# PSUM banks by lists, another order of maxima, and six smaller moves in a transformer block of one core

## The chip, the cores and the metric

The kernel runs on one core of a Trainium2 chip. The metric is the time of one execution in device microseconds (us), as the median of several runs. TensorE (PE) multiplies matrices into PSUM, which has eight banks of 128 rows by 512 float32; VectorE (DVE) and ScalarE (ACT) read PSUM; GpSimd (POOL) works on SBUF alone; SyncE (SP) issues the DMAs from one queue.

## The reference

One block of a transformer in float32 for 2048 tokens of width 640: layer norm and attention with 32 heads of 20, then layer norm and a gated feed-forward layer of width 1728, both with a residual.

```python
h  = x + attention(layernorm(x), wqkv, wo)   # qkv = z @ wqkv; softmax(q k^T / sqrt(20)) v; @ wo
h2 = h + (silu(z2 @ w_gate) * (z2 @ w_up)) @ w_down   # z2 = layernorm(h)
```

## The kernel before

Tokens go in 4 chunks (`NC`) of 512, each of 4 tiles of 128. Products are exact in two parts: `split` writes the high part of a tensor with ScalarE (`hi`, type fp32r) and the rest with another engine (`lo`); three products `hi*hi`, `hi*lo`, `lo*hi` are added. The program's order on each engine is written out by the Python code; there is no scheduler behind it. All waits between engines follow from which tiles are read and written.

**First phase, projections.** For each chunk `c` the work list has "block" steps (128 columns of q or k, 15 products twice, once for each half of 64 rows of the array, which run side by side) and "value" steps. Each step has a number, the slot; `begins(c)` is the first slot of a chunk, and the list has 72 slots. Between the products the planner `Halves` places *pairs*: parts of the row maxima of q k^T, which attention needs before it takes exponentials. They lie in two lists. `early` holds maxima of units 2, 4, 5, 8 and so on that can be had from the projected chunks; `others` holds those of units 0 and 1. A unit `u` is 4 heads (`g = u // 4`) by one chunk of queries (`c = u % 4`), 32 units in all. `staged_keys` makes 8 pairs for a set with one key tile and 16 for one with two; `early` gets 240 pairs and `others` 48, in the order unit 0, unit 1, unit 0, unit 0. A set's keys and queries are loaded back from DRAM into free places, those of `others` in a lane of their own (`lane=1`) with two places. `next_pair` says which list is asked first. When the last pair of unit 0 is issued, `over` calls `max_all(0)` (DVE L242, POOL L246 and L247); `max_finish(0)` (PE L254, ACT L258, four DMAs L263) writes the maxima as two more rows of the queries. It runs two slots after that (`finish_at`), or, where the list of slots ends before, behind `pe.drain()` and the last load of values (L170). `norm(c)` makes the layer norm of a chunk (L720 applies it), `flip` transposes it (L745).

**Attention.** For each unit, 16 key tiles. `ORDER` is the order of one tile: `s` and `S` are scores of a head in the lower and upper half of the array (L1336, then the exponential, L1342, on ScalarE), `m` and `M` a maximum of a later unit (L229 and DVE L235), `W` the weighing of the tile before (`weigh`, L1346), which uses four strips of 32 columns. Steps of other work stand behind `W`: weight preparation, and in the last two units the output projection of chunks 0 and 1 (`projection`; its parts: `part`, L89, splits the attention output `o_t` into `o_hi` and `o_lo`; `project`, L1070, 15 products of 128x320, added to `h` at L1076; `apply`, L1090; `flip`, L1102, five transposes, then `split`). Its PSUM comes from `ps_max`, three banks. The planner knows when maxima end (`closing`), so that `max_finish(u)` comes some tiles before unit `u`.

**After attention.** The last unit's sums are normalised: ACT L1356 copies the accumulator, a reciprocal (L1367), `r_d` and back as `rb`, a product (L1381), stores to `o_d`. Meanwhile chunk 2 is projected (`two`), then chunk 3 (`three`), which loads `o_d` again. Then the feed-forward layer runs over 14 weight blocks (`ELEMENTS`) for two pairs of chunks: `blocks` gives the gate and up products (L1514) of PSUM `ps_a`; between its 8 steps, `next_down` issues the down projection of earlier blocks (L1608, PSUM `ps_b`), a `Group` of 7 or 4 products at a time. `prepare` splits a group's input into `yp`, one of three buffers. `late_tokens` normalises, transposes (L1861, L1878) and stores chunks 2 and 3, one item a step.

PSUM is handed out by tile pools, closed and opened again at four places: `psum_f` (the first transposes), `psum` (first phase: `ps_one` 3 banks, `ps_single` 5), `psum_a` (attention: `ps_one` 4, `ps_max` 3, `acc` 1), `psum2` (`ps_b` 4, `ps_a` 4).

Of the kernel before, what the change touches and what calls it, by code (L numbers as in the profile page):

```python
# [17 lines left out]
P = 128  # L18
# [22 lines left out]
MARGIN = 0.2  # L41
LAST_QUARTER = 60
# [5 lines left out]
def tile_block(ctx: ExitStack, tc: tile.TileContext, x, wqkv, wo, wg, wu, wd, out):  # L48
# [20 lines left out]
    ps_ctx = ExitStack()  # L69
    psum = ps_ctx.enter_context(tc.tile_pool(name="psum_f", bufs=1, space=bass.MemoryType.PSUM))  # L70
    wides, ones = 3, 1

    def ps_wide():
        return psum.tile([P, 2, CH], F32, name="ps_wide", tag="ps_wide", bufs=wides)

    def ps_one():
        return psum.tile([P, CH], F32, name="ps_one", tag="ps_one", bufs=ones)

    def ps_single():
        return psum.tile([P, CH], F32, name="ps_single", tag="ps_single", bufs=5)  # L80
# [248 lines left out]
    with tc.tile_pool(name="pa", bufs=2) as pa:  # L329
# [184 lines left out]
        class Halves:  # L514
# [32 lines left out]
            def issue(self, half):  # L547
# [3 lines left out]
                if half == 0 and i == 0:  # L551
                    del self.ones[0]
                    job["ps"] = ps_one()
# [14 lines left out]
                if job["at"][1] == job["n"]:  # L568
                    self.jobs.remove(job)
                    self.ones.append(job["done"](job["ps"]) + 0.2)  # L570
# [143 lines left out]
        def norm(c):  # L714
# [4 lines left out]
            def apply(t):  # L719
                (nc.gpsimd if c else nc.vector).tensor_scalar(  # L720
# [10 lines left out]
                + [(("pool", 1.3), lambda t=t: apply(t), c) for t in range(TPC)]  # L731
# [137 lines left out]
        ps_ctx.close()  # L869
        ps_ctx = ExitStack()  # L870
        psum = ps_ctx.enter_context(tc.tile_pool(name="psum", bufs=1, space=bass.MemoryType.PSUM))
        ones = 3
# [118 lines left out]
    ps_ctx.close()  # L991


    ps_ctx = ExitStack()
    psum = ps_ctx.enter_context(tc.tile_pool(name="psum_a", bufs=1, space=bass.MemoryType.PSUM))

    def ps_one():
        return psum.tile([P, CH], F32, name="ps_one", tag="ps_one", bufs=4)

    def ps_max():  # L1000
        return psum.tile([P, CH], F32, name="ps_max", tag="ps_max", bufs=3)
# [36 lines left out]
    def projection(c, ps_of):  # L1038
# [17 lines left out]
        def part(t):  # L1056
# [3 lines left out]
            split(o, o_hi, o_lo, nc.gpsimd)  # L1060
            loaded[t] = (o_hi, o_lo)

        def project(t, half):
            o_hi, o_lo = loaded[t]
            hs = slice(half * HALF, (half + 1) * HALF)
            ps = ps_of()
            n = 0
# [981 lines left out]
```

## Time and profile before

| | |
|---|---|
| median of 3 runs | 2039.87 us (2039.75 to 2042.74) |
| the profiled execution | 2035.66 us, span of its instructions 2033.9 us |
| TensorE busy | 2008.8 us (99%) |
| VectorE, ScalarE, GpSimd busy | 1612.6, 1462.4, 785.7 us |
| mean granted TensorE clock | 0.997 |
| first phase, to the first score at | 328.1 us |
| attention, to the last weighing at | 1470.1 us |
| DMA | 305.03 MB, mean 150 GB/s |

Times in the profile are from the first instruction. A busy TensorE is not TensorE at its peak: its matmuls are pipelined, and their ends are modelled. Rows of the timeline read: start, duration, engine, line, operation, output<-input, shape, count, and in brackets the idle time of the engine just before and what ended it. Rows of waits read: who waited, for whom, total us, times, longest.

### The profile page before, as it was taken

The numbers are of one execution on the slowest core, as the hardware profiler recorded it, in microseconds if no ns is written. First come the engines' busy times: TensorE is split into PE (matmuls) and PEld (weight loads), VectorE is DVE, ScalarE is ACT, GpSimd is POOL, SyncE is SP. The second block draws the span as 40 slices with busy tenths as digits, with TensorE's granted clock in tenths as the row PEclk, the third lists the DMA queues.
The fourth block names the chain that finished last, engine by engine and source line by source line (L and its number), as shares of the span: only waits on it lengthen the run. The fifth ranks groups of instructions, "written<-read, shape, count | busy, mean of one in ns | idle before, by whom it ended". The sixth has DMA issues, their size and how long they took to land. (4 is left out here: it accounts for less than half of the span.)

```text
span 2033.9 us, 39129 instructions
## 1 busy us (share of the span) xinstructions
PE 2008.8 (99%) x13716; PEld 1238.9 (61%) x13716; DVE 1612.6 (79%) x3241; ACT 1462.4 (72%) x2952; POOL 785.7 (39%) x1079
## 2 busy tenths in 40 slices
PE   7999999999999999999999999999999999999999
PEld 6899996333333333333333333345598888888888
DVE  6678788888888888888888888885377666676677
ACT  3788988999999999999999999987633222211221
POOL 5554450334434334344430011011145454744555
PEclk9999999999999999999999999999999999999999
DMA  7776663343443534444433123211158654974642
GB/s 227 243 222 186 203 185 100 113 128 99 150 124 113 163 123 138 129 141 146 141 126 109 30 65 80 83 62 49 41 193 292 222 193 156 346 272 159 202 151 95
DMA packets 205124, 305.03 MB, mean 150 GB/s; under 512 B 47664, under 2 KB 82480, under 8 KB 203904
## 3 DMA queue, kind: packets, MB, share of 16 engines
q1 hardware_dynamic: 204832, 302.53, 45.9%
q8 instruction: 109, 1.79, 0.4%
q14 instruction: 87, 0.71, 0.1%
q10 hardware_dynamic: 96, 0.00, 0.0%
HBM read 205.78 MB, written 95.68 MB: 148 GB/s over the span
## 5 line engine op out<-in xcount | busy, mean ns | idle before, releaser
L1342 ACT ACTIVATE probs<-ps_one 128x512 f32<-128x512 f32 x2048 | 1056.9, 615 | 62.0 <-PE ps_one L1336 24.2
L235 DVE TENSOR_REDUCE mx<-ps_max 128x1 f32<-128x512 f32 x1472 | 925.4, 684 | 116.2 <-PE ps_max L229 64.1
L1336 PE MATMUL ps_one<-q_stk,k_stk 62*128 62x512 f32 x2048 | 583.5, 431 | 1.2 <-DVE mx L199 1.2
L1346 PE MATMUL acc<-probs,v_stk 128*32 128x512 f32 x4096 | 546.7, 605 | 0.0
L229 PE MATMUL ps_max<-k_stk,q_stk 60*128 60x512 f32 x1472 | 488.7, 440 | 0.1
L1336 PEld LDWEIGHTS ps_one<-q_stk,k_stk 62*128 62x128 f32 x2048 | 290.5, 185 | 284.7 <-ACT probs L1342 269.7
L229 PEld LDWEIGHTS ps_max<-k_stk,q_stk 60*128 60x128 f32 x1472 | 245.2, 185 | 165.4 <-DVE mx L235 126.9
L1729 DVE TENSOR_TENSOR tmp<-ps_a,tmp 128x512 f32<-128x512 f32 x208 | 141.3, 690 | 122.1 <-PE ps_a L1514 96.4
L1346 PEld LDWEIGHTS acc<-probs,v_stk 128*32 128x32 f32 x4096 | 80.6, 108 | 181.7 <-issue 169.5
L1608 PE MATMUL ps_b<-halves,yp 128*128 128x320 f32 x1032 | 179.0, 308 | 1.5 <-POOL yp L89 1.3
L1608 PEld LDWEIGHTS ps_b<-halves,yp 128*128 128x128 f32 x1032 | 165.2, 188 | 17.5 <-POOL yp L89 1.5
L1514 PE MATMUL ps_a<-t,units 128*128 128x512 f32 x624 | 162.5, 396 | 0.0
L246 POOL CAST both<-neg 128x16 fp32r<-128x16 f32 x32 | 6.6, 207 | 361.6 <-PE ps_one L1336 153.7
L1514 PE MATMUL ps_a<-z,units 128*128 128x512 f32 x516 | 133.9, 394 | 0.0
L89 POOL TENSOR_TENSOR yp<-y,yp 128x256 fp32r<-128x256 f32 x96 | 60.2, 627 | 189.8 <-ACT yp L88 189.8
L1514 PEld LDWEIGHTS ps_a<-t,units 128*128 128x128 f32 x624 | 112.6, 188 | 18.5
L1613 DVE TENSOR_TENSOR h<-ps_b,h 128x320 f32<-128x320 f32 x248 | 110.0, 482 | 6.9 <-PE ps_b L1608 5.4
L216 DVE CUSTOM_DVE_ANT_0 q_stk<-ps_single,q_stk 128x512 f32<-128x512 f32 x143 | 95.7, 689 | 22.4 <-ACT q_stk L222 15.0
L1514 PEld LDWEIGHTS ps_a<-z,units 128*128 128x128 f32 x516 | 93.1, 187 | 16.0
L556 PE MATMUL ps_one<-z_hi,w_hi 64*128 64x512 f32 x380 | 99.1, 402 | 1.8 <-ACT z_hi L88 1.7
L88 ACT ACTIVATE yp<-tmp 128x512 fp32r<-128x512 f32 x40 | 25.3, 632 | 103.2 <-POOL tmp L1601 103.2
L1381 POOL TENSOR_TENSOR o<-o,rb 128x512 f32<-128x512 f32 x31 | 39.9, 1286 | 152.9 <-ACT probs L1342 55.8
(221 smaller groups left out, 3017.9 us busy)
## 6 DMA issues: line engine op xcount, KB each, us to landing
units<-w_d SPq DMA_DIRECT2D x186, 256.0 KB
w_d<-stage SPq DMA_DIRECT2D x106, 256.0 KB
halves<-j_d SPq DMA_DIRECT2D x70, 320.0 KB
k_stk<-qk_d SPq DMA_DIRECT2D x112, 160.0 KB
j_d<-stage SPq DMA_DIRECT2D x42, 320.0 KB
q_stk<-qk_d SPq DMA_DIRECT2D x64, 160.0 KB
k_stk<-qk_d SPq DMA_DIRECT2D x112, 80.0 KB
rb<-r_d SPq DMA_DIRECT2D x32, 256.0 KB
```

The lines of the kernel that those rows point to most:

```text
L89: lo_engine.tensor_tensor(out=lo, in0=src, in1=hi.bitcast(F32), op=ALU.subtract)
L216: nc.vector.tensor_tensor_reduce(out=place, in0=pss[1], in1=place, scale=1.0, scalar=LEAST, op0=ALU.add, op1=ALU.max, accum_out=mx[:, b, p ...
L229: nc.tensor.matmul(ps, queries[u][rows, pair, t * P : (t + 1) * P], keys[u // NC][rows, pair, kc * CH : (kc + 1) * CH], start=True, stop=True,
L235: nc.vector.tensor_reduce(mxs[u][:, b, pair, t, kc : kc + 1], ps, axis=AX.X, op=ALU.max)
L556: product = nc.tensor.matmul(job["ps"][:, :out], lhs, rhs, start=(half == 0 and i == 0), stop=(half == 1 and i == job["n"] - 1),)
L1336: nc.tensor.matmul(ps, keys[u // NC][rows, p, kt * P : (kt + 1) * P], queries[u][rows, p, :], start=True, stop=True,)
L1342: nc.scalar.activation(probs[p][:, b, :], ps, AF.Exp, scale=scale)
L1346: nc.tensor.matmul(acc[32 * j : 32 * j + 32, :], values[u // NC][:, kt, j * VW : j * VW + 32], probs[j // 2][:, j % 2, :], start=(kt == 0) ...
L1514: nc.tensor.matmul(ps.rearrange("p (t n) -> p t n", t=TPC), w[k][:, i], z[k][:, :, j], start=(first and m == 0), stop=(last and m == len(n ...
L1608: nc.tensor.matmul(ps, a, b, start=(n == 0), stop=(n == len(pairs) - 1))
L1613: nc.vector.tensor_tensor(out=h, in0=ps, in1=h, op=ALU.add)
L1729: add = lambda out, ps, x: nc.vector.tensor_tensor(out=out, in0=ps, in1=x, op=ALU.add)
```

## The change

1. One PSUM tile `banks` of eight banks lives through the kernel. Lists say which banks a use has: `wide_places`, `one_places`, `single_places`, later `max_places` and `acc_place`. A use takes the next of its list (`turn`); a projection step takes a bank and gives it back when done. The four pools are gone.
2. `next_pair` asks `others` first where `others` has more than a quarter (`SHARE = 4`) as many pairs as `early`, in place of a fixed slot.
3. The second chunk's layer norm is applied by VectorE instead of GpSimd, and the planner's cost of GpSimd's is 2.55 instead of 1.3. `place`, which fills the unused rows of a free place, reads `w_hi` instead of `k_stk`.
4. The first tile of attention has no maxima (order `sSsSW`), so that all maxima come one tile later.
5. In the last unit the projection (of chunk 1) is done in two halves of 64 rows, in two banks, the second half two products behind (`BEHIND`), and added twice; and the weighing is done for two tiles at a time, at even tiles.
6. For chunks 2 and 3, `o_lo` is made by VectorE instead of GpSimd. For chunk 1, VectorE and not ScalarE copies the transposes' high part.
7. Late tokens are normalised two steps before their transposes, and take 5 steps a tile instead of 6. Three groups are prepared ahead instead of two. The last token tile is stored in two halves.

```diff
+BEHIND = 2
+SHARE = 4
...
+    psum = ctx.enter_context(tc.tile_pool(name="psum", bufs=1, space=bass.MemoryType.PSUM))
+    banks = psum.tile([P, 8, CH], F32, name="banks")
+    wide_places, one_places, single_places = [2, 4, 6], [0, 1, 2], [3, 4, 5, 6, 7]
+    def turn(places):
+        places.append(places.pop(0))
+        return places[-1]
     def ps_one():
-        return psum.tile([P, CH], F32, name="ps_one", tag="ps_one", bufs=ones)
+        return banks[:, turn(one_places)]
...
         def place(t):
-            ones = k_stk[0][:, 1, S - 2 * CH :]
             for b in range(2):
-                rows = slice(b * ROW + NPART, (b + 1) * ROW)
-                nc.sync.dma_start(t[rows].bitcast(F32), ones[rows].bitcast(F32))
+                some = w_hi[b * ROW + NPART : (b + 1) * ROW].rearrange("r k c -> r (k c)")[:, : 2 * CH]
+                rows = t[b * ROW + NPART : (b + 1) * ROW]
+                nc.sync.dma_start(rows.bitcast(F32), some.bitcast(F32))
...
-            queues = (others, early) if slot[0] >= begins(NC - 1) else (early, others)
+            queues = (others, early) if len(others) * SHARE > len(early) else (early, others)
...
-                (nc.gpsimd if c else nc.vector).tensor_scalar(
+                (nc.gpsimd if c > 1 else nc.vector).tensor_scalar(
...
+    a, b, c, *max_places = single_places
+    one_places.append(b)
+    max_places, acc_place = [a, c, max_places[0]], max_places[1]
     def ps_max():
-        return psum.tile([P, CH], F32, name="ps_max", tag="ps_max", bufs=3)
+        return banks[:, turn(max_places)]
...
-            split(o, o_hi, o_lo, nc.gpsimd)
+            split(o, o_hi, o_lo, nc.gpsimd if c < 2 else nc.vector)
...
+            rows = [slice(b * ROW, (b + 1) * ROW) for b in range(2)] if halved else [slice(0, P)]
+            pss = [ps_of() for _ in rows]
+            terms = ((o_hi, wo_hi), (o_hi, wo_lo), (o_lo, wo_hi))
+            for n in range(3 * ND + BEHIND * (len(rows) - 1)):
+                for i, (r, ps) in enumerate(zip(rows, pss)):
+                    m = n - BEHIND * i
+                    if 0 <= m < 3 * ND:
+                        (a, w), k = terms[m // ND], m % ND
+                        nc.tensor.matmul(ps[:, :HALF], a[r, k, :], w[r, k, hs], ...)
             h = h_c[c][:, t, hs]
-            nc.vector.tensor_tensor(out=h, in0=ps[:, :HALF], in1=h, op=ALU.add)
+            for ps in pss:
+                nc.vector.tensor_tensor(out=h, in0=ps[:, :HALF], in1=h, op=ALU.add)
...
+                if c == 0:
+                    split(src, hi, lo, nc.vector)
+                else:
+                    nc.vector.tensor_copy(hi, src)
+                    nc.vector.tensor_tensor(out=lo, in0=src, in1=hi.bitcast(F32), op=ALU.subtract)
...
-            order = ORDER[now[0] % len(ORDER)] if singles[0] or singles[1] else "sSsSW"
+            order = ORDER[now[0] % len(ORDER)] if now[0] and (singles[0] or singles[1]) else "sSsSW"
...
-                    if todo:
-                        weigh_next()
+                    both = u == NU - 1 and kt < NT - 1
+                    for _ in range(2 * (1 - kt % 2) if both else 1):
+                        if todo:
+                            weigh_next()
...
-                        c - 1, ps_max if c < NC - 1 else (lambda: ps_b())
+                        c - 1, ps_max if c < NC - 1 else (lambda: ps_b()), c == NC - 2
...
+            tt = self.c * TPC + self.t + i
+            first = HALF if tt == NT - 1 else 0
-            if self.fs[0] == NF - 2 and half == 1:
+            if self.fs[0] == NF - 2 and (half == 1 or first):
...
-        for g in waiting[:2]:
+        for g in waiting[:3]:
             g.prepare()
...
-        items = moments() + [lambda: apply(2, 0)]
+        items = moments() + [lambda: apply(2, 0), lambda: apply(3, 0)]
         items.append(store)
+        items.append(lambda: flip(2, 0))
         for t in range(TPC):
-            items.append(lambda t=t: (store(), apply(3, t), flip(2, t)))
-            items.append(
-                lambda t=t: (store(), t + 1 < TPC and apply(2, t + 1), flip(3, t))
-            )
-            items.append(lambda: (store(), sums()))
-            items.append(store)
-            items.append(lambda t=t: (store(), keep(zz[2], t_d[0], t)))
-            items.append(lambda t=t: (store(), keep(zz[3], t_d[1], t, nc.vector)))
+            more = t + 1 < TPC
+            items += [
+                lambda t=t, more=more: (store(), more and apply(2, t + 1), flip(3, t)),
+                lambda t=t, more=more: (store(), sums(t), more and apply(3, t + 1)),
+                lambda t=t, more=more: (store(), more and flip(2, t + 1)),
+                lambda t=t: (store(), keep(zz[2, t], t_d[0], t)),
+                lambda t=t: (store(), keep(zz[3, t], t_d[1], t, nc.vector)),
+            ]
```

More of the change, by code (lines that the diff above doesn't have):

```diff
@@ L552, in issue @@
                     del self.ones[0]
-                    job["ps"] = ps_one()
+                    job["place"] = one_places.pop(0)
+                    job["ps"] = banks[:, job["place"]]
                 rows = slice(half * ROW, (half + 1) * ROW)
@@ L730, in norm @@
                 + [(("vector", 0.35), lambda f=f, g=g: (f(), g()), c) for f, g in zip(steps[::2], steps[1::2] + [lambda: None])]
[L731 removed]
+                + [
+                    (("pool", 2.55) if c > 1 else ("vector", 0.75), lambda t=t: apply(t), c)
+                    for t in range(TPC)
+                ]
             )
@@ L1407, in weigh_next @@
         if kt == 0:
-            accs[u] = psum.tile([P, CH], F32, name="acc", tag="acc", bufs=1)
+            accs[u] = banks[:, acc_place]
         weigh(u, kt, probs, accs[u])
@@ L1490, in tile_block @@
     att_ctx.close()
-    ps_ctx.close()
-    psum2 = ctx.enter_context(tc.tile_pool(name="psum2", bufs=1, space=bass.MemoryType.PSUM))
+    max_places.append(acc_place)
     def ps_b():
-        return psum2.tile([P, CH], F32, name="ps_b", tag="ps_b", bufs=4)
+        return banks[:, turn(one_places)]
     pe2 = ctx.enter_context(tc.tile_pool(name="pe2", bufs=1, side="right"))
@@ L1694, in bank @@
     def bank():
-        return psum2.tile([P, CH], F32, name="ps_a", tag="ps_a", bufs=4)
+        return banks[:, turn(max_places)]
     def gated(ps):
```

48 lines of the change are left out of this document (17 added, 31 removed).

## The prediction

> **What bounds the kernel now.** I read the page first, then what TensorE waited for, then stretches of a few microseconds around each wait, and last the timeline inside them.
>
> ```profile
> span 2033.9 us, 39129 instructions
> PE 2008.8 (99%) x13716; PEld 1238.9 (61%) x13716; DVE 1612.6 (79%) x3241; ACT 1462.4 (72%) x2952; POOL 785.7 (39%) x1079
> ...
> PE ps_a L1878 <- DVE z L1861: 2.3, 2, 1.2
> ...
> PE ps_one L788 <- DVE z_lo L89: 1.6, 1, 1.6
> PE ps_single L745 <- POOL xt L720: 1.6, 1, 1.6
> PE ps_b L1608 <- POOL yp L89: 1.3, 1, 1.3
> PE ps_one L1336 <- DVE mx L199: 1.2, 1, 1.2
> PE ps_b L1070 <- ACT o L1356: 0.7, 1, 0.7
> ```
>
> TensorE is busy 99% of the span: 25 us are open in all, and no more than about 9 of them stand in these waits (columns: total, times, longest). The change can earn those, the time lost to a lowered clock behind them, and whatever TensorE loses inside "busy" time.
>
> ```profile
> 44.00:48.00 4.00, 4.00 (x39) 3.96 (x38) 1.46 (x3) 1.86 (x3) 4.00 (x4) 1.00 0.58 183
> 48.00:52.00 4.00, 2.43 (x26) 2.15 (x24) 0.38 (x1) 0.80 (x3) 4.00 (x2) 1.00 0.71 195
> 52.00:55.50 3.50, 3.50 (x21) 3.35 (x19) 1.55 (x8) 2.70 (x7) 3.50 (x4) 0.52 0.60 164
> ...
> 325.00:328.50 3.50, 2.03 (x10) 0.90 (x9) 2.79 (x16) 2.25 (x8) 0.00 (x0) 1.00 0.29 115
> 328.50:332.00 3.50, 3.50 (x18) 1.77 (x18) 3.33 (x6) 3.31 (x7) 0.00 (x0) 0.52 0.54 161
> 332.00:335.40 3.40, 3.40 (x15) 1.20 (x11) 1.29 (x3) 1.31 (x4) 0.00 (x0) 0.50 0.12 37
> 335.40:339.00 3.60, 3.60 (x26) 1.28 (x27) 2.84 (x5) 3.42 (x7) 0.00 (x0) 0.99 0.00 0
> ```
>
> Each row gives busy time and count of PE, PEld, DVE, ACT and POOL, then the granted clock. Twice a stretch with 1.5 us of idle TensorE is followed by one at clock 0.5: around 50 (projections of the second chunk) and around 327 (from projections to attention). Those two places are worth more than their waits.
>
> **A, PSUM by lists.** Bank counts per use stay as they are (four for scores, three for maxima, one accumulator), so steady attention is costed at nothing. What goes is the wait of a new pool for the old one's last reader.
>
> ```profile
> 15.33 0.70 ACT L88 ACTIVATE z_hi<-ps_wide 128x640 fp32r<-128x640 f32 x1 [0.53 <-PE ps_wide L763]
> ```
>
> At the start the first ten products need only z_hi, written at 16.03, but began after z_lo, 1.65 after their engine fell idle; they gain 0.8. z_lo and w_lo are due ten and twenty products later and are there.
>
> **B, second chunk normalised on VectorE.**
>
> ```profile
> 45.27 5.48 POOL L720 TENSOR_SCALAR xt<-xt,mv,r_a 128x640 f32<-128x640 f32 x2
> 11.08 2.18 DVE L720 TENSOR_SCALAR xt<-xt,mv,r_a 128x640 f32<-128x640 f32 x4
> ```
>
> GpSimd ends its four at 50.75, and TensorE's transposes wait 1.6 for it. VectorE does four in 2.2, and was busy 1.46 of 4 us there: done by about 43. The wait goes. The half clock behind it issued 21 instructions in 3.5 us where the row of 44 to 48 gives 34: 13 at 9.75 per us, 1.3 us, which goes too if the idle stretch is its cause. B is 2.9. The page "TensorE: Matmul & The Clock Gate" of the Trainium skill ("Why this matters for your kernels") says the clock falls behind gaps over some 3 us. By it a gap of 1.6 would not be the cause, and B would be 1.6. The two drops of this trace, each right behind a shorter gap, speak against it. Next late are the maxima on VectorE and ScalarE, whose pairs fill this phase; I let them take back 0.75 of A and B's 3.7.
>
> **C, queue order and the first tile.** By the code, `early` starts with 240 pairs and `others` with 48; all maxima of unit 0 are in `others`, its last eight at the very end. Today `others` goes first from slot 46 on, and unit 0 is closed long before it is used:
>
> ```profile
> 271.72 0.22 DVE L242 TENSOR_REDUCE neg<-mx 128x16 f32<-128x64 f32 x1
> 278.80 2.80 SPq L263 DMA_DIRECT2D q_stk<-m  x4
> 319.56 6.38 SPq L305 DMA_DIRECT2D v_d<-ev  x2
> 328.06 0.37 SPq L170 DMA_DIRECT2D v_stk<-v_d  x1
> 328.69 4.03 ACT L1342 ACTIVATE probs<-ps_one 128x512 f32<-128x512 f32 x8 [1.39 <-PE ps_max L229]
> ...
> L199 DVE CUSTOM_DVE_ANT_0 q_stk<-ps_single,q_stk 128x256 f32<-128x256 f32 x16 | 5.8, 420 | 0.9 <-ACT q_stk L197 0.9
> ```
>
> With SHARE 4, `others` goes first only while it holds over a quarter of `early`, so its last pair comes when fewer than four of `early` are left: in the last 3 us of the phase, at the 0.7 a pair of its end (16 L199, two a pair, in 5.8). `finish_at` is two slots later, behind the loop, so `max_finish(0)` falls behind the drain, and its DMAs stand on SP's queue behind the last v_stk load. That one waits for v_d's store to land, 2.1 after its issue ended at 325.94, and is out at 328.43. The four DMAs take 2.80 (two serve one half of the rows); landing as the store did, they are there at 331.9 and 333.3. Scores, which wait for them, began at 328.10 today. So they start 3.8 later, and the other half 1.4 behind (0.7 on average). Against it: TensorE now idles through the first half-clock stretch instead of working in it. Today those 6.9 us issued 33 instructions where 7.2 per us (26 in 3.6) would have given 50, a loss of 2.3; half of it (1.2) goes, and the first tile without its three maxima saves 0.8 at half clock. C is 3.8+0.7-1.2-0.8 = +2.5. Bounds: if pairs end in time, the pool's wait (1.2) and most of the dip (2.0) go, -3.2; if the dip lasts another 3.4 us, +4.5. Later maxima all move by one tile; each unit's are still closed some tiles before its scores, at no cost (at most +1, in the last unit). `place` reading w_hi instead of k_stk moves no queue: nothing.
>
> **D, the last unit.**
>
> ```profile
> 1429.20 0.76 PE L1336 MATMUL ps_one<-q_stk,k_stk 62*128 62x512 f32 x4
> 1429.89 1.07 PE L1346 MATMUL acc<-probs,v_stk 128*32 128x512 f32 x8
> 1430.89 1.00 PE L1070 MATMUL ps_max<-wo_hi,o_hi 128*128 128x320 f32 x5
> 1433.29 0.76 PE L1336 MATMUL ps_one<-q_stk,k_stk 62*128 62x512 f32 x4
> ...
> 1461.74 2.06 ACT L1342 ACTIVATE probs<-ps_one 128x512 f32<-128x512 f32 x4
> 1464.28 2.15 ACT L1342 ACTIVATE probs<-ps_one 128x512 f32<-128x512 f32 x4
> 1466.19 0.90 ACT L88 ACTIVATE z<-ps_max 128x512 fp32r<-128x512 f32 x2
> 1466.94 0.89 DVE L89 TENSOR_TENSOR z<-ps_max,z 128x512 fp32r<-128x512 f32 x2 [1.21 <-ACT z L88]
> 1473.18 0.90 PE L1070 MATMUL ps_b<-wo_hi,o_hi 128*128 128x320 f32 x5
> 1475.38 0.90 PE L1070 MATMUL ps_b<-wo_hi,o_hi 128*128 128x320 f32 x5
> ```
>
> Eight tiles are TensorE's: 4.09 each, 0.69 scores, 1.00 weighing, 2.40 projection. Three changes of array shape cost some 0.2 each (an estimate from the 2.40 against 2.20 for the same fifteen, 1473.18 to 1475.38, with no change of shape). Halves have the scores' shape, and double weighing leaves two changes per two tiles instead of six: -0.8, and +0.3 for the two steps that one half trails; -2.0 over four pairs. One weighing (1.00) also moves out of them: -3.0. The second addition (0.5 on an idle VectorE) is hidden. The other eight tiles are ScalarE's, 2.06 for four exponentials. Two weighings hold TensorE about 1.9; with some 0.4 of scores before them and as much again until the next scores are out, ScalarE waits 2.7 to 2.9 with 2.06 of work in its four banks, and runs dry for about 0.75 in each of four pairs: +3.0. Copies that leave ScalarE for VectorE (0.90 a tile) bring 2.54 a tile (1461.74 to 1464.28) down only to VectorE's own 2.35 (0.89, as much for the copies, 0.55 for z as in L720's row), and unblock the first: -1.2. D is -1.2, from -4.2 (no starving) to +2.
>
> **E, the end of attention and o_lo on VectorE.**
>
> ```profile
> 33.69 0.78 DVE L89 TENSOR_TENSOR w_lo<-raw,w_hi 128x640 fp32r<-128x640 f32 x1
> 1475.53 0.49 DVE L1076 TENSOR_TENSOR h<-ps_b,h 128x320 f32<-128x320 f32 x1 [5.08 <-DMA h<-in_A_x]
> 1476.85 0.90 PE L1070 MATMUL ps_b<-wo_hi,o_lo 128*128 128x320 f32 x5
> 1494.61 0.74 ACT L88 ACTIVATE o_hi<-o_t 128x640 fp32r<-128x640 f32 x1 [5.95 <-DMA o_t<-o_d]
> 1495.59 0.90 PE L1070 MATMUL ps_b<-wo_hi,o_hi 128*128 128x320 f32 x5
> ```
>
> The wait on ScalarE's o goes (-0.7). But o_lo now stands on VectorE behind the first sum, which waits for x until 1475.53: sum, statistics (a half each) and o_lo (0.78) end at about 1477.4, and TensorE, 0.7 earlier now than 1476.85, wants it by 1476.2. Then the reciprocal, behind two o_lo of 0.78, comes 1.6 later, and with it the chain over r_d, rb, o_d and o_t to the last o_hi at 1494.61, which has 0.2 to spare before 1495.59. E is +1.3 (-0.6 if VectorE's queue is shorter than I count, +2.2 with the chain wholly behind).
>
> **F, late tokens two steps ahead.** The two waits of L1878, 2.3, go: z is two steps old when transposed. Three steps fewer cost the same instructions closer together, on ScalarE and GpSimd with room. -2.3, to 0.
>
> **G, three groups prepared.** yp's wait of 1.3 goes with a chance of three in four, -1.0; a third tile held in three buffers can add 0.5.
>
> **H, last store in halves.**
>
> ```profile
> 2030.06 0.49 DVE h L1613
> ```
>
> The last sum starts at 2030.06; with it, an issue and a landing the span ends 3.8 later; half the bytes save 0.3, 0 to 0.6.
>
> **Sum.** A -0.8, B -2.9, given back +0.75, C +2.5, D -1.2, E +1.3, F -2.3, G -1.0, H -0.3: -4.0. The profiled execution took 2035.66 around its span of 2033.9, and would take 2031.7. The median of the runs is 2039.87, 4.2 above it; the same 4.0 off gives 2035.9. A measurement of this kernel tells about 0.2%, 4.1 us, from no change: the forecast lies at that edge.
>
> **Rivals.** *The pairs end in time* (22%): the mixed order keeps both lists fed, everything is drained two slots early, and C is -3.2. For it, VectorE and ScalarE have some idle time through the phase; against, the list rule itself. Sum -9.7: 2030.2. *The last keys of unit 0 come last of all* (16%, slower): lane 1 has two places, the set before the last holds both, and the last chunk is loaded only when that set ends. If `early` has run down to under ten by then, TensorE idles through a load and a landing (about 5, as v_d's store and four DMAs above) and then eight pairs at about 0.7, the drain pace, before C's chain: 8 to 10 on top, of which some 1.5 overlaps; 2043. It decides where the load ends against `early`'s last pair. *The maxima hold the first phase* (19%): A and B are given back whole, or the clock drops have another cause, as the skill's page would have it: -1 to -2.5, 2038. The forecast itself: 43%.
>
> **Numbers.** The forecast's own range is ±3, half of it beyond 4.1: faster 0.22+0.22 = 0.44, same 0.21+0.19 = 0.40, slower 0.16. The range runs from the first rival, 2029.7, to 2043.8, which takes in half of the second.
>
> **What would show it.** L720 for the second chunk on DVE, no wait at 50 and clock 1.0 to 55 (B). L263 for unit 0 as the last issues before the scores, and ACT's first L1342 near 332 less A and B (C); if L242's first row lies 10 us or more before the first scores, C is wrong. Last unit: projection tiles alternating near 2.7 and 5.0, ScalarE gaps of about 0.8 in its second half (D). L1367 later behind o_lo, and a wait at the second L1070 block (E). No L1878 wait (F). A wait over 8 us on raw<-qk_d near the end of the first phase would mean the slower rival.

## The result and the profile after

The changed kernel takes 2092.66 us (2089.26 to 2094.30, five runs); the kernel before took 2039.75 beside it (2036.57 to 2042.74, five runs). The ratio is 1.0258, 95% interval 1.0240 to 1.0275: 53 us slower, where 4 us faster was forecast, and outside the range. The profiled execution took 2089.44.

The page of the changed kernel, its first lines and two groups of instructions (busy, mean ns | idle before, releaser):

```profile
span 2087.6 us, 39199 instructions
...
PE 2022.9 (97%) x13836; PEld 1249.2 (60%) x13836; DVE 1627.2 (78%) x3266; ACT 1463.9 (70%) x2943; POOL 769.2 (37%) x1070
...
L1622 PE MATMUL banks<-halves,yp 128*128 128x320 f32 x1032 | 183.7, 312 | 25.8 <-ACT yp L96 13.0
...
L96 ACT ACTIVATE yp<-y 128x256 fp32r<-128x256 f32 x96 | 31.0, 364 | 158.3 <-DVE y L1749 86.6
```

TensorE has 64.7 us open instead of 25.1, and 14.1 us more "busy" time. What it waited for (total, times, longest):

```profile
PE banks L1622 <- ACT yp L96: 13.0, 4, 3.5
PE banks L1622 <- DVE own L1645: 9.4, 3, 3.1
PE banks L1350 <- DMA q_stk<-m: 8.3, 1, 8.3
...
PE banks L1622 <- DVE own L1643: 3.1, 1, 3.1
PE banks L1528 <- ACT tmp L1758: 2.6, 1, 2.6
...
PE banks L1079 <- DVE o_lo L97: 1.2, 1, 1.2
...
PE banks L1350 <- ACT probs L1356: 0.9, 2, 0.5
```

The down products (L1622, L1608 before) wait eight times for 3.1 to 3.5 us; before, they waited once, 1.3. The first scores (L1350) wait 8.3. The waits on the late tokens (L1878 before) and on the second chunk's transposes (L745 before) are gone, as forecast. There is also a new wait of 2.6 in the gate and up products (L1528). By stretches of the two profiled executions (times of first and last instructions in them):

| stretch | before | after | difference |
|---|---|---|---|
| to the first score | 328.1 | 337.6 | +9.5 |
| first score to last weighing | 1142.0 | 1144.1 | +2.1 |
| last weighing to last product with wo | 43.3 | 44.5 | +1.2 |
| from there to the last down product | 516.6 | 556.0 | +39.5 |
| from there to the end | 3.9 | 5.3 | +1.4 |

So three quarters of the loss lie in the feed-forward part, where the change, besides the bank lists, does two things: the late tokens' order (F) and three prepared groups (G). The timeline shows how a wait there comes about; rows of ACT, POOL, DVE and PE in the changed kernel ahead of the first:

```profile
1642.31 0.69 DVE L1745 TENSOR_TENSOR tmp<-banks,tmp 128x512 f32<-128x512 f32 x1
1642.80 0.63 ACT L96 ACTIVATE yp<-tmp 128x512 fp32r<-128x512 f32 x1 [2.46 <-POOL tmp L1615]
1643.34 0.60 ACT L96 ACTIVATE yp<-y 128x256 fp32r<-128x256 f32 x2
...
1645.45 0.46 POOL L1612 TENSOR_TENSOR tmp<-y 128x128 f32<-128x128 f32 x1
...
1646.82 0.45 POOL L1615 TENSOR_TENSOR tmp<-y,tmp 128x128 f32<-128x128 f32 x1
...
1647.31 0.63 ACT L96 ACTIVATE yp<-tmp 128x512 fp32r<-128x512 f32 x1 [3.37 <-POOL tmp L1615]
1647.85 0.61 ACT L1789 ACTIVATE tmp<-tmp 128x512 f32<-128x512 f32 x1
1648.37 0.58 ACT L1758 ACTIVATE tmp<-banks 128x512 f32<-128x512 f32 x1
1648.49 1.34 DVE L1749 TENSOR_TENSOR y<-tmp 128x512 f32<-128x512 f32 x1 [5.49 <-ACT tmp L1789]
...
1649.92 0.62 ACT L96 ACTIVATE yp<-y 128x256 fp32r<-128x256 f32 x2 [0.98 <-DVE y L1749]
1650.33 1.14 PE L1622 MATMUL banks<-halves,yp 128*128 128x320 f32 x3 [3.52 <-ACT yp L96]
```

And the same place in the kernel before:

```profile
1625.83 0.69 DVE L1729 TENSOR_TENSOR tmp<-ps_a,tmp 128x512 f32<-128x512 f32 x1
...
1626.32 0.63 ACT L88 ACTIVATE yp<-tmp 128x512 fp32r<-128x512 f32 x1 [2.45 <-POOL tmp L1601]
1626.86 0.61 ACT L1773 ACTIVATE tmp<-tmp 128x512 f32<-128x512 f32 x1
...
1627.50 1.36 DVE L1733 TENSOR_TENSOR y<-tmp 128x512 f32<-128x512 f32 x1 [0.98 <-ACT tmp L1773]
```

When a block's first half is done, two groups come to the list at once. With two prepared, the second of them waits for a later step. With three, its splits are issued at once, and ScalarE's queue holds a rounding (L96, yp<-tmp) that needs four sums of GpSimd, which has the first group's work in front of it. ScalarE stands 3.37 us. Behind it in the queue is the Silu of the second half (L1789): its input was ready at 1643.00, it starts at 1647.85. So y is late, its split is late, and the down products run out. In four of the eight waits the profile names a split (yp) as the last to come, in the other four a sum on VectorE (`own`). ScalarE is 70% busy in all and nowhere near the bound here; it is the order of its queue that costs. The page "Perfetto Trace Analysis" of the Trainium skill (section "Tensor Engine Instruction") says that ScalarE, VectorE and GpSimd execute strictly first in, first out; the rows agree: the ready Silu stood 4.85 us.

### The profile page after: what moved, and what is told of

Same layout as the page of the kernel before. It is cut to its first block, busy times and chain, and to the rows that moved or that the text cites. A ratio compares the mean times of both kernels' runs of the same rounds, so it can differ in the third digit from the quotient of the medians.

```text
span 2087.6 us, 39199 instructions
## 1 busy us (share of the span) xinstructions
PE 2022.9 (97%) x13836; PEld 1249.2 (60%) x13836; DVE 1627.2 (78%) x3266; ACT 1463.9 (70%) x2943; POOL 769.2 (37%) x1070
## 4 chain that ended last, share of the span: by engine, by line
PE 74%; POOL 3%; DVE 3%; DMA 2%; ACT 1%; issue 1%; SPq 0%; DVEq 0%; ACTq 0%; POOLq 0%
PE banks L1360 24%; PE banks L1350 16%; PE banks L1528 12%; PE banks L237 11%; PE banks L1622 6%; PE banks L1079 2%; POOL yp L97 1%; DVE y L1749 1%; ACT yp L96 1%; DVE tmp L1745 1%; POOL tmp L1613 0%; POOL tmp L1612 0%; POOL tmp L1615 0%; POOL tmp L1614 0%; DMA halves<-j_d 0%
## 5 line engine op out<-in xcount | busy, mean ns | idle before, releaser
L1356 ACT ACTIVATE probs<-banks 128x512 f32<-128x512 f32 x2048 | 1056.1, 612 | 72.2 <-PE banks L1350 27.4
L243 DVE TENSOR_REDUCE mx<-banks 128x1 f32<-128x512 f32 x1472 | 924.9, 684 | 124.7 <-PE banks L237 77.4
L1350 PE MATMUL banks<-q_stk,k_stk 62*128 62x512 f32 x2048 | 584.1, 430 | 9.2 <-DMA q_stk<-m 8.3
L1360 PE MATMUL banks<-probs,v_stk 128*32 128x512 f32 x4096 | 547.2, 608 | 0.0
L237 PE MATMUL banks<-k_stk,q_stk 60*128 60x512 f32 x1472 | 487.1, 439 | 0.2
L1350 PEld LDWEIGHTS banks<-q_stk,k_stk 62*128 62x128 f32 x2048 | 293.0, 185 | 292.6 <-ACT probs L1356 269.6
L237 PEld LDWEIGHTS banks<-k_stk,q_stk 60*128 60x128 f32 x1472 | 244.5, 184 | 163.0 <-DVE mx L243 126.0
L1622 PE MATMUL banks<-halves,yp 128*128 128x320 f32 x1032 | 183.7, 312 | 25.8 <-ACT yp L96 13.0
L1622 PEld LDWEIGHTS banks<-halves,yp 128*128 128x128 f32 x1032 | 167.9, 191 | 44.3 <-issue 14.0
L1528 PE MATMUL banks<-t,units 128*128 128x512 f32 x624 | 164.1, 398 | 2.8 <-ACT tmp L1758 2.6
L96 ACT ACTIVATE yp<-y 128x256 fp32r<-128x256 f32 x96 | 31.0, 364 | 158.3 <-DVE y L1749 86.6
L1528 PE MATMUL banks<-z,units 128*128 128x512 f32 x516 | 139.6, 407 | 1.0 <-DVE tmp L1745 1.0
L1528 PEld LDWEIGHTS banks<-t,units 128*128 128x128 f32 x624 | 113.3, 189 | 22.3 <-ACT tmp L1758 2.9
L1528 PEld LDWEIGHTS banks<-z,units 128*128 128x128 f32 x516 | 97.3, 196 | 18.2 <-DVE tmp L1745 1.2
L96 ACT ACTIVATE yp<-tmp 128x512 fp32r<-128x512 f32 x40 | 25.3, 632 | 107.7 <-POOL tmp L1615 107.7
```

The source lines that it names most:

```text
L237: nc.tensor.matmul(ps, queries[u][rows, pair, t * P : (t + 1) * P], keys[u // NC][rows, pair, kc * CH : (kc + 1) * CH], start=True, stop=True,
L243: nc.vector.tensor_reduce(mxs[u][:, b, pair, t, kc : kc + 1], ps, axis=AX.X, op=ALU.max)
L1350: nc.tensor.matmul(ps, keys[u // NC][rows, p, kt * P : (kt + 1) * P], queries[u][rows, p, :], start=True, stop=True,)
L1356: nc.scalar.activation(probs[p][:, b, :], ps, AF.Exp, scale=scale)
L1360: nc.tensor.matmul(acc[32 * j : 32 * j + 32, :], values[u // NC][:, kt, j * VW : j * VW + 32], probs[j // 2][:, j % 2, :], start=(kt == 0) ...
L1528: nc.tensor.matmul(ps.rearrange("p (t n) -> p t n", t=TPC), w[k][:, i], z[k][:, :, j], start=(first and m == 0), stop=(last and m == len(n ...
```

## Three groups (G): three runs

Two prepared, the rest of the change left in:

```diff
-        for g in waiting[:3]:
+        for g in waiting[:2]:
```

> The changed kernel with two groups prepared instead of three, and all else of the change left in. Theory Q (head of the queue): preparing the third group puts a split of its sums on ScalarE's queue ahead of the next Silu; ScalarE stands on GpSimd's four sums, the Silu comes 4.9 us late, so y and its split are late and the down products of the next group wait 3.1 to 3.5 us, eight times, each followed by some 2 us of a lower clock. Without it all eight waits are gone and 35 to 42 us of the 53 come back: 2051 to 2058. Rival L (late tokens or the new bank lists set those waits): the eight waits stay and the time is 2088 to 2095.

Measured: 2046.25 us, ratio to before 1.0041 (1.0026 to 1.0057). All eight waits of over 3 us are gone and the 2.6 with them, and one of 1.25 on yp is there, as before the change. 46.4 us come back by the medians (44.9 when each is taken from the kernel before that ran beside it), more than expected; by the profiles, 41.5 in the stretch to the last down product (556.0 to 514.5). Windows of that stretch, with three groups and with two:

```profile
1526.28:2082.31 556.03, 526.47 (x2666) 455.96 (x2665) 366.89 (x705) 121.07 (x256) 276.70 (x396) 0.98 0.58 196
```

```profile
1527.06:2041.54 514.48, 512.87 (x2667) 446.94 (x2665) 366.30 (x705) 119.47 (x256) 275.94 (x396) 1.00 0.62 212
```

TensorE is idle for 29.6 us there instead of 1.6, and busy for 13.6 us more with the same products. The trace with three groups has six stretches at half clock in this window, 27.3 us in all, and the one with two has none; half of 27.3 is the busy time that is lost. So the waits make two thirds of G's price and the lowered clock the rest.

The reverse, three prepared in the kernel before:

```diff
-        for g in waiting[:2]:
+        for g in waiting[:3]:
```

> The kernel before with three groups prepared instead of two, and nothing else of the change. Theory Q: the eight waits of 3.1 to 3.5 us appear here too and the time is 2075 to 2082. Rival L: it needs the change's other parts, and the time stays at 2038 to 2042. If three groups were worth what the prediction said, 2038 to 2039.

Measured: 2078.90 us, ratio 1.0204 (1.0177 to 1.0231). Page and group rows:

```profile
span 2078.5 us, 39094 instructions
...
L1608 PE MATMUL ps_b<-halves,yp 128*128 128x320 f32 x1032 | 184.8, 314 | 26.5 <-ACT yp L88 13.0
```

The same eight waits with nothing else of the change. Late tokens and bank lists have no part in them, as theory Q says.

Three prepared, but nothing on ScalarE's queue waits for GpSimd's sums:

```diff
-            split(x, p[:, 0, 3:], p[:, 1, 3:], nc.gpsimd)
+            nc.gpsimd.tensor_copy(p[:, 0, 3:], x)
+            tt(out=p[:, 1, 3:], in0=x, in1=p[:, 0, 3:].bitcast(F32), op=ALU.subtract)
```

> The changed kernel, three groups prepared, but the high half of each group's four sums is rounded by GpSimd and no longer by ScalarE, so nothing on ScalarE's queue waits for GpSimd's sums; GpSimd gets 40 casts of about 0.75 us more (a cast of 128x256 took 0.38 us). Theory Q: the Silu is no longer late, the eight waits vanish or fall under 1 us, 2050 to 2060. Rival R (GpSimd's chain of sums and splits for two groups in a row is itself what the products wait for): the waits grow by 0.7 to 1.5 us each, 2095 to 2106.

Measured: 2046.76 us, ratio 1.0042 (1.0028 to 1.0056). Groups of this kernel:

```profile
L1623 PE MATMUL banks<-halves,yp 128*128 128x320 f32 x1032 | 178.7, 308 | 0.2 <-DVE h L1628 0.2
...
L1617 POOL CAST yp<-tmp 128x512 fp32r<-128x512 f32 x40 | 25.9, 647 | 0.0
```

That is under the 2050 to 2060 of theory Q. GpSimd does 25.9 us more, and the down products wait 0.2 us in all. So the chain on GpSimd is not what they waited for: it is the place in ScalarE's queue. Here the third group also gives what the forecast wanted of it: the wait of 1.25 that two groups leave is gone, and the stretch is 513.0 instead of 514.5.

## The first phase (B and C): four runs

In the changed kernel the first scores wait for the last row of unit 0's maxima; rows of the timeline:

```profile
327.15 0.22 DVE L250 TENSOR_REDUCE neg<-mx 128x16 f32<-128x64 f32 x1
...
327.52 0.20 POOL L254 CAST both<-neg 128x16 fp32r<-128x16 f32 x1 [4.01 <-DVE neg L250]
...
329.08 0.25 PE L262 MATMUL banks<-ones_r,both 128*32 128x128 f32 x1
...
329.70 0.26 ACT L266 ACTIVATE m<-banks 32x128 fp32r<-32x128 f32 x1
329.85 0.34 SPq L313 DMA_DIRECT2D v_d<-ev  x1
330.28 1.71 SPq L161 DMA_DIRECT2D k_stk<-qk_d  x4
332.60 0.39 SPq L178 DMA_DIRECT2D v_stk<-v_d  x1
333.08 2.81 SPq L271 DMA_DIRECT2D q_stk<-m  x4
...
337.63 1.72 PE L1350 MATMUL banks<-q_stk,k_stk 62*128 62x512 f32 x4 [8.30 <-DMA q_stk<-m]
```

That is term C's chain (L271, behind the last load of values L178). From the end of the projections to the first score it takes 8.5 us instead of 3.1; the forecast has 3.8 more, and 5.4 are measured. The old rule for pairs should undo it:

```diff
-            queues = (others, early) if len(others) * SHARE > len(early) else (early, others)
+            queues = (others, early) if slot[0] >= begins(NC - 1) else (early, others)
```

> As the kernel with two groups, and the rule for taking pairs is also the old one (the second queue goes first only from the last chunk's blocks on). Theory C: the maxima of unit 0 end early again, its last DMAs stand no longer behind the last loads, the first scores start at 328 to 329 us instead of 337.6, and the time is 8 to 10 us under that of the kernel with two groups: 2042 to 2049. Rival V (the wait comes from the VectorE work that the second chunk's normalising and the lists move, not from the order of the pairs): the first scores stay at 335 to 338 us and the time is within 2 us of the kernel with two groups.

Measured: 2046.51 us, ratio 1.0044 (1.0029 to 1.0059): nothing gained on 2046.25. The 8.2 us wait is gone, but the first scores start at 336.3. Windows of this kernel (PE, PEld, DVE, ACT, POOL busy; granted clock):

```profile
308.18:321.83 13.65, 12.55 (x126) 11.63 (x122) 9.75 (x31) 9.86 (x20) 4.28 (x5) 1.00 0.88 231
321.83:342.31 20.48, 19.78 (x59) 12.35 (x61) 16.05 (x61) 16.54 (x36) 5.32 (x2) 0.50 0.18 59
```

The projections end at 319.8, 5.2 us earlier than before, but 41 pair products are left behind them (3 before), TensorE issues them at the pace of VectorE and ScalarE until 336.8, and from 321.83 on all of it runs at half clock. Theory C fell: its wait went, and its gain did not come. Rival V's two numbers came out (first scores at 335 to 338, the time within 2 us), but not its reason for the wait, which went with the rule. The pairs are placed by the planner, which counts with the prices that it is given; the second chunk's normalising is now an entry of VectorE, and later ones cost 2.55 on GpSimd. By the count in the expectation below, 23 pairs are left for the drain instead of 8. So B has to go back with C:

```diff
-                (nc.gpsimd if c > 1 else nc.vector).tensor_scalar(
+                (nc.gpsimd if c else nc.vector).tensor_scalar(
...
-                + [
-                    (("pool", 2.55) if c > 1 else ("vector", 0.75), lambda t=t: apply(t), c)
-                    for t in range(TPC)
-                ]
+                + [(("pool", 1.3), lambda t=t: apply(t), c) for t in range(TPC)]
```

> The kernel with two groups, with the second chunk's normalising back on GpSimd at its old price in the plan and the old rule for pairs: the plan then issues the pairs in the order of the kernel before (8 left for the drain; with the rule alone put back 23 were left, since the two parts act on one plan). Theory P (the two parts cost the first phase some 9 us only through the order of the pairs that the plan makes of them): the first scores start at 327 to 329 us, and the time is 7.5 to 10 us under that of the kernel with two groups. Rival B (the lists of PSUM banks slow the first phase by themselves): the first scores stay at 333 us or later and the time gains under 5 us.

Measured: 2037.99 us, ratio 0.9999 (0.9990 to 1.0009). The projections end at 324.3 with 3 pair products behind, the first scores start at 325.6, even earlier than theory P has it. The lists of banks cost the first phase nothing. With the first phase back, the whole kernel stands where the one before stood. The new rule alone, B undone:

```diff
-            queues = (others, early) if slot[0] >= begins(NC - 1) else (early, others)
+            queues = (others, early) if len(others) * SHARE > len(early) else (early, others)
```

> The kernel with two groups, the second chunk's normalising back on GpSimd at its old price, but the new rule for pairs kept: against the kernel with both old (2037.99) this is the new rule alone. The plan leaves 5 pairs and the last of unit 0 for the drain. Theory C: the chain behind unit 0's last pair and its DMAs come after the last loads, the first scores wait 7 to 9 us on them with some 10 us at half clock behind, and the time is 2045 to 2048. Rival M (it takes the normalising on VectorE as well): the first scores start by 330 us and the time is within 2 us of 2038.

Measured: 2046.49 us, ratio 1.0038 (1.0024 to 1.0052); the first scores start at 337.8 after a wait of 7.7 on q_stk<-m. So the new rule alone costs 8.5 us (2046.49 to 2037.99), the normalising alone 8.5 (2046.51 to 2037.99), and both together 8.3 (2046.25): each spoils the end of the phase in a way of its own. (Taken from the kernel before that ran beside each, it is 7.7, 8.6 and 8.3.) No run separates the two parts of that edit, the engine that does it and the new prices in the plan. The new rule mends what the normalising does to the pairs (no pair products are left behind the projections), only to hold the last ones of unit 0 back.

One try to have both, `others` in any case first from slot 60 on:

```diff
-            queues = (others, early) if len(others) * SHARE > len(early) else (early, others)
+            queues = (others, early) if len(others) * SHARE > len(early) or slot[0] >= 60 else (early, others)
```

> The kernel with two groups, the second chunk's normalising on VectorE and the new rule kept, but from slot 60 of the first phase on the second queue goes first in any case. The plan then leaves 6 pairs of the first queue and none of the second for the drain (4 and 1 in the changed kernel), and the maxima of unit 0 are done some 20 us before it. Theory C (the 8.2 us wait is the chain behind the last pair of unit 0: its reduction, GpSimd's cast, the transposition, the copy and the DMAs behind the last loads): the wait goes, the first scores start at 328 to 331 us, the time falls 7 to 11 us against the kernel with two groups. Rival V (VectorE is late with its pairs whatever the order): the first scores start at 334 us or later, and the time falls by under 4 us.

Measured: 2050.15 us, ratio 1.0058 (1.0043 to 1.0073). Neither C's time nor V's late start came. The scores do start at 330.0, and then a maximum stops; a row of TensorE's waits, and one of SP's timeline:

```profile
PE banks L237 <- DMA k_stk<-qk_d: 7.0, 2, 6.5
```

```profile
331.56 3.27 SPq L161 DMA_DIRECT2D k_stk<-qk_d  x8
```

The keys' own buffer lends quarters as places for staged pairs (L161 loads the keys into them afterwards). Pairs that run to the end hold them to the end: eight loads go out at 331.56, where the kernel with the old first phase issued its last before 312. Only the chain named in the expectation went; another load had been behind it.

## The last unit (D) and o_lo (E): two runs

Tiles weighed singly again, beside the last kernel:

```diff
-                    both = u == NU - 1 and kt < NT - 1
+                    both = False
```

> As the kernel whose second queue goes first from slot 60 on, but the last unit weighs one tile a time as the other units do (the last projection's halves stay). Theory D: weighing two tiles at every other tile leaves TensorE without work for 0.45 us twice while ScalarE makes four exponentials in a row, and two stretches of 3.4 us at half clock follow, which costs 3.4 us; weighed singly the last unit ends 2 to 4 us earlier and the time falls as much. Rival H (the halves of the projection cost it, or the doubling saves what was hoped for): the last unit ends no earlier, the time stays or rises by up to 3 us.

Measured: 2046.21 us, ratio 1.0034 (1.0022 to 1.0046), 3.9 us under 2050.15. The last two units in one window each, of the kernel with slot 60 (doubled) and of this one (single):

```profile
1369.80:1482.40 112.60, 111.07 (x833) 63.46 (x829) 63.31 (x141) 75.48 (x149) 14.81 (x12) 0.98 0.15 47
```

```profile
1372.10:1480.70 108.60, 108.11 (x833) 60.74 (x829) 62.95 (x140) 75.45 (x149) 14.84 (x12) 1.00 0.16 49
```

The stretch is 110.8 in the kernel before, 108.6 here, 112.6 doubled, and 114.2 in the changed kernel. There the windows show why:

```profile
1458.70:1462.12 3.42, 2.97 (x13) 1.12 (x16) 2.29 (x10) 2.95 (x7) 0.00 (x0) 1.00 0.00 0
1462.12:1465.53 3.41, 3.41 (x20) 0.93 (x12) 0.00 (x0) 1.07 (x3) 0.00 (x0) 0.50 0.00 0
1465.53:1468.95 3.42, 2.96 (x16) 1.02 (x16) 0.00 (x0) 3.22 (x7) 0.00 (x0) 1.00 0.02 5
1468.95:1472.36 3.41, 3.41 (x17) 1.14 (x9) 0.00 (x0) 1.42 (x3) 0.00 (x0) 0.50 0.00 0
```

Behind each wait of 0.45 us stands a stretch at half clock here. That is not so in every execution: all eight kernels with doubled weighing have the two waits, and they had two such stretches (114.2 to 114.3), one (112.5 to 112.7) or none (110.9, the kernel with the new rule alone): 1.7 us each, half of 3.41, over some 2.3 for the starving itself. The last units of the four kernels that weigh singly in halves take 108.5 to 108.6, with neither the waits nor a lowered clock.

The low half on GpSimd:

```diff
-            split(o, o_hi, o_lo, nc.gpsimd if c < 2 else nc.vector)
+            split(o, o_hi, o_lo, nc.gpsimd)
```

> As the kernel whose second queue goes first from slot 60 on, but the low half of the last two chunks' split is on GpSimd again. Theory E: the wait of 1.07 to 1.2 us that TensorE has there on VectorE's o_lo goes and nothing else takes its place; the last projection's last matmul ends about 1 us earlier and the time falls 0.5 to 1.5 us. Rival G (GpSimd's 1.57 us a piece is later than VectorE's queue): the wait stays or grows to 2 us, and the time stays or rises by up to 1 us.

Measured: 2048.12 us, ratio 1.0046 (1.0031 to 1.0061), 2.0 under 2050.15, more than theory E has, with runs that overlap (2045.91 to 2050.17 and 2048.08 to 2053.11). The wait shows it: 0.36 on GpSimd is left of 1.05 on VectorE, and all eight kernels with o_lo on VectorE have one of 1.0 to 1.2. The stretch from the last weighing to the last product with wo is 43.0 instead of 44.2, but it is a weak witness: the kernel before and the one with nothing but three groups have the same code up to there, and take 43.3 and 44.5. In the changed kernel the wait is, as the forecast has it, VectorE's queue behind the load of x:

```profile
1487.23 0.49 DVE L1085 TENSOR_TENSOR h<-banks,h 128x320 f32<-128x320 f32 x1 [4.87 <-DMA h<-in_A_x]
...
1488.17 0.81 DVE L97 TENSOR_TENSOR o_lo<-o_t,o_hi 128x640 fp32r<-128x640 f32 x1
...
1489.03 1.00 PE L1079 MATMUL banks<-wo_hi,o_lo 128*128 128x320 f32 x5 [1.20 <-DVE o_lo L97]
```

## What is left when the losing parts go: three runs

The old first phase, single weighing, o_lo on GpSimd and three groups with GpSimd's own rounding; kept are bank lists, halves, the late tokens' order and the divided store. Against the kernel with the old first phase:

```diff
-            split(o, o_hi, o_lo, nc.gpsimd if c < 2 else nc.vector)
+            split(o, o_hi, o_lo, nc.gpsimd)
...
-                    both = u == NU - 1 and kt < NT - 1
+                    both = False
...
-            split(x, p[:, 0, 3:], p[:, 1, 3:], nc.gpsimd)
+            nc.gpsimd.tensor_copy(p[:, 0, 3:], x)
+            tt(out=p[:, 1, 3:], in0=x, in1=p[:, 0, 3:].bitcast(F32), op=ALU.subtract)
...
-        for g in waiting[:2]:
+        for g in waiting[:3]:
```

> What the runs so far speak for, together: the first phase in its old order (the second chunk's normalising on GpSimd at its old price, the old rule for pairs), tiles weighed singly in the last unit, the low half of the last chunks' split on GpSimd, three groups with the high half of their sums rounded by GpSimd; kept are the bank lists, the last projection's halves, the late tokens' order and the divided last store. By the earlier traces this should be worth, against the kernel with the first phase in its old order (2037.99): single weighing 3.4 to 4.2, the split 0.8 to 1.5, the wait of 1.2 us that three groups remove in the MLP. Theory S (these add up): 2031 to 2034, ratio 0.997 to 0.998 to the kernel before. Rival N (they hide one another): 2036 to 2038.

Measured: 2032.89 us, ratio 0.9969 (0.9957 to 0.9980): the parts add up, as theory S has it.

From there, the last store in one piece:

```diff
-            first = HALF if tt == NT - 1 else 0
+            first = 0
```

> As the kernel of the parts together, but the last row of tokens is stored in one piece again. Theory T: the two halves of 160 KB cost rather than gain, since the store queue is busy to the end (the stretch from the last matmul to the end of the span was 3.9 us before and 4.7 to 5.6 us in all kernels with the divided store); with one piece that stretch is 3.8 to 4.2 us, but the last matmul comes no earlier, so the time falls 0.5 to 1.5 us. Rival U (the stretch is longer only because the stores before it start together and end at the same moment whatever the last one does): it stays at 4.7 us or more, and the time within 0.4 us.

Measured: 2030.49 us, ratio 0.9957 (0.9945 to 0.9970), the fastest kernel here. Its page:

```profile
span 2027.7 us, 39225 instructions
...
PE 2004.4 (99%) x13836; PEld 1239.3 (61%) x13836; DVE 1617.9 (80%) x3257; ACT 1439.7 (71%) x2904; POOL 812.7 (40%) x1119
```

The stretch behind the last down product is 5.2 us against 5.5 with the divided store, so the longer stretch stays, as rival U has it, though the time does not; the 2.4 us between the medians lie elsewhere: in the two profiled executions the first scores start at 327.4 and 330.8, with the same code up to there. (In all six executions with the old first phase they start anywhere from 325.6 to 330.8.) Whether the divided store costs anything stays open; it brought nothing that could be seen.

From the kernel of the parts together again, the late tokens in the old order, one step ahead:

```diff
-        items = moments() + [lambda: apply(2, 0), lambda: apply(3, 0)]
+        items = moments() + [lambda: apply(2, 0)]
...
-        items.append(lambda: flip(2, 0))
...
-                lambda t=t, more=more: (store(), more and apply(2, t + 1), flip(3, t)),
-                lambda t=t, more=more: (store(), sums(t), more and apply(3, t + 1)),
-                lambda t=t, more=more: (store(), more and flip(2, t + 1)),
...
+            items.append(lambda t=t: (store(), apply(3, t), flip(2, t)))
+            items.append(
+                lambda t=t: (store(), t + 1 < TPC and apply(2, t + 1), flip(3, t))
+            )
+            items.append(lambda t=t: (store(), sums(t)))
+            items.append(store)
...
```

> As the kernel of the parts together, but the late tokens are normalised and turned in the old order, one step ahead. Theory F (the forecast's): the two waits of 1.24 and 1.09 us on VectorE's z return and the time rises by 1.9 to 2.4 us. Rival K (the waits return but later slack takes them up): the time rises by under 0.6 us.

Measured: 2031.70 us, ratio 0.9968 (0.9955 to 0.9980): no difference to 2032.89 in the medians, whose runs spread over 6 to 7 us. The two waits are back with 1.17 and 1.00, and the stretch from the last product with wo to the last down product is 514.7 instead of 512.7. By the traces F is worth 2.0, as theory F has it; the medians can't show so little.

## Why the prediction was wrong, point by point

- **G** is the step that failed. It was costed by the buffers alone ("a third tile held in three buffers can add 0.5") and put at -1.0. Of the splits that it issues, it did not ask on which queue they stand and who is behind: measured +41.5 in the profile, 28 of it in waits and the rest in a lowered clock, for which it had no term. The rows of L88 in the trace of before (yp<-tmp, 103.2 us of ScalarE's idle time put down to GpSimd's tmp) were there to be read.
- **B** (-2.9): the wait at 50 went, but TensorE then waits at the same place 1.3 and 0.4 for loads, and the changed kernel has a stretch of 3.41 us at half clock of its own at 69.49. Its 1.3 of clock was one execution's: six others of the kernels run here have the same wait of 1.6 there, and none has the half clock there. The kernel with the old first phase, window of the forecast's row:

```profile
52.00:55.50 3.50, 3.50 (x34) 3.26 (x32) 1.46 (x7) 3.44 (x10) 3.50 (x4) 1.00 0.71 179
```

  The give-back of 0.75 is the term that was mis-sized: moving an entry of the plan, with new prices that the forecast does not mention, moved all pairs, 8.5 us with the old rule.
- **C** (+2.5): right chain, right direction. The price of the new rule alone was 8.5. Mis-sized was the chain (5.4 for 3.8). Missed were a phase that ends 4.1 later (329.15 instead of 325.05; one execution with the old first phase ends it as late, at 329.4) and 10.2 us of half clock where the forecast saw the dip grow shorter. The four loads of keys at 330.28 are new in the chain but cost little: from the store's issue to the load of values it takes 2.4 us, and 2.1 before. Counting terms one at a time also failed: B and C act on one plan.
- **D** (-1.2): the mechanism is right. Halves and copies bring 2.2 (108.6 to 110.8; forecast 3.2; they were not undone singly, and bank lists and the later maxima are in it too), doubled weighing costs 2.3 before the clock (forecast 3.0 less 1.0). The clock, up to 3.4, was not in the sum, and puts D at +3.4 in the changed kernel (110.8 to 114.2), beyond its bound of +2.
- **E** (+1.3): the wait on VectorE's o_lo is as forecast, 1.2. The sum is not shown: the stretch averages 44.2 in eight kernels with o_lo on VectorE and 43.6 in six with it on GpSimd, and the latter spread over 1.5. **F** (-2.3): right, 2.0 to 2.3.
- **A** (-0.8): the wait at the start went from 1.65 to 0.79. **H** (-0.3): wrong; the stretch behind the last down product is longer by 1.4 (3.9 to 5.3). With the store in one piece it is still 5.2, so most of that comes from elsewhere, and no run shows from where.
- The rivals: "pairs end in time" and "the last keys come last" did not happen; the slower rival had a price near the first phase's loss (8 to 10) by another way. No rival had the feed-forward part in it: the trace of before shows the down products waiting there 1.3 us, and the late tokens 2.3. (The forecast's lower end, 2029.7, does not fit its first rival's sum, which is 2030.2.)

## What to carry to other kernels

Work that is prepared further ahead is only free if each engine's queue that it enters has nothing more urgent behind it: before raising a look-ahead, list its instructions per engine, what each waits for, and the next instruction of the critical chain on that engine. Where a planner places work by prices, a changed price is a changed program: count what is left over at its end before costing the edit. And a stretch can be more sensitive than a median, if executions of the same code agree on it: the one to the last down product is 514.0 to 514.6 in seven kernels that differ only elsewhere, so 2 us can be read there, while the start of the first scores differs by 5 us with the same code.

## What was not expected of the hardware

All stretches of half clock in the fourteen traces last 3.41 us or a multiple (6.83, 10.24, 13.65, 20.48), but for those that the end of an execution cuts short, and their starts in one execution lie on a grid of that step (1462.12, 1468.95 and 1612.31 in the changed kernel are 2 and 42 steps apart). Of the eight waits of 3.1 to 3.5 us in the changed kernel, five have such a stretch beginning in or right behind them. So have one of the seven waits of 1.6 at the second chunk's transposes, and ten of the sixteen of 0.40 to 0.46 in the eight kernels with doubled weighing. The page "TensorE: Matmul & The Clock Gate" of the Trainium skill (section "Part 1: The HAM clock gate") has the clock decided by a free-running window of about 3.4 us, and the grid agrees with it; the length of a gap alone, by which the forecast weighed its two cases, does not decide it here. What the window counts is not shown by these runs: TensorE was busy for 2.97 of the 3.42 us ahead of one drop.
